# Turning q and k on VectorE in 32x32 blocks of bf16 pairs, and scores as four 32-row tiles of two half products

## Chip, cores and metric

The kernel runs on one core of one Trainium2 chip. The metric is device time in microseconds from start to end of one execution; lower is better. A core has five engines that run at the same time and wait for each other through semaphores: PE (TensorE, matrix products, with its weight loads shown apart as PEld), DVE (VectorE), ACT (ScalarE), POOL (GpSimd) and SP (SyncE, which here only issues DMAs).

## What is computed

Attention with a decay bias for 8 batches of 8 heads (576 positions, head width 64), then a token mixer and a channel mixer. `s` gives the decay. Cut to what matters:

```python
scores = scale * np.matmul(q, k.transpose(0, 1, 3, 2))        # q, k, v: (8, 8, 576, 64)
bias = -(cum[:, :, :, None] - cum[:, :, None, :])             # cum = cumsum(max(s, 0))
scores = np.where(causal, -1e9, scores + np.minimum(bias, 0.0))
attn = softmax(scores)
x = (attn @ v), heads side by side                            # (8, 576, 512)
h = np.maximum(x.T @ w_tok1, 0.0) @ w_tok2                    # 576 -> 256 -> 576
u = x + h.T
out = u + np.maximum(u @ w_ch1, 0.0) @ w_ch2                  # 512 -> 1536 -> 512
```

The kernel uses that the decay makes far keys negligible: each block of 128 queries meets only its own block of keys and the one before. Where a check at the end finds that the inputs do not allow this, a slower general path would run.

## The kernel before

**Units of work.** A batch has two *quads* of four heads. For each quad, k and q are loaded (L560), cast to bf16 (L573, on POOL in the steady part), turned so that the head width lies on partitions, and multiplied. A quad's four heads make two *pairs*. For each pair: two score blocks on PE (L650), an exponential on ACT for each block (L655, out of a PSUM tile of two banks, 128x1024 values), a causal mask on DVE (L660, L668), and two times nine small products with v (L685), a reciprocal (L692) and a scaling (L697) into `x`. When `x` of a batch is complete, the token mixer (L752, L773, with the addition L780) and the channel mixer (L826, the relu L833 or L835, L844, the addition L855) follow. From the third batch on, `u` is turned by a DMA transpose that SP issues (L789); for the first two batches PE turns it (L798).

**How q and k are turned.** PE does it: nine 128x128 transposes (L613) put k, then q, of a quad into a score tile of PSUM, and ACT (L623) or DVE (L625) copies each half out. Two heads of 64 rows then lie above each other in `kT` and `qT`, so a score block runs as two products of 64 rows at a time on the two halves of the array, each with the whole head width.

**What sets the order.** The kernel writes out its instructions through a planner of its own (class `Plan`, L47 to L202). Each operation is given a cost for each engine that may do it, a priority, the buffers it needs and what it waits for. The planner goes through time and picks for each engine the operation that can start first, by priority where several can. What it picks is the order of the instructions on that engine; on the chip each engine goes through its list in order. Buffers come from rings of few tiles: two PSUM tiles `psc` of two banks for scores, three `E` tiles, four `qkf` tiles for loads, two `qkn` tiles for casts. Loads are issued by SP in a fixed order among themselves (L419 to L421), between them the stores of the output (L860, L863) and the DMA transposes.

**Fills.** Where the planner leaves PE idle in its first 95 us, products with a zero tile are put in (L930), so that PE stays at work until the weights are there.

**Squares.** At the end a flag needs the sum of squares of q and k. For batches 2 to 7 it is taken from the cast tiles on ACT (L587), for batches 0 and 1 from a second load late in the run (L597).

Of the kernel before, what the change touches and what calls it, by code (L numbers as in the profile page):

```python
# [46 lines left out]
class Plan:  # L47
# [47 lines left out]
    def run(self, eps=0.03):  # L95
# [17 lines left out]
        def slot_time(o):  # L113
            t = 0.0
            want = {}
            for b in o.bufs:
                if b.slot is None:
                    r = b.ring
                    if b.ordered and r.queue[0] is not b:
                        return None  # L120
                    fr = [r.free[i] for i in range(len(r.tiles)) if not r.busy[i]]
                    if not fr:
                        return None
                    t = max(t, min(fr))
                    want[id(r)] = want.get(id(r), 0) + 1
            return t
# [207 lines left out]
def kernel(  # L334
# [12 lines left out]
    nc = tc.nc  # L347
# [13 lines left out]
    R = 9  # L361
    PR = S // R

# [29 lines left out]

    r_qf = ring("qkf", 4, [128, 2, R, D], FP32)
    r_qn = ring("qkn", 2, [128, 2, R, 2, D], BF16)
    r_qT = ring("qT", 2, [128, 2, S], BF16)
    r_kT = ring("kT", 2, [128, 2, 640], BF16)
# [21 lines left out]
    def load_op(fn, key, us):  # L419

        last[0] = P.op({"SP": (0.6, 0, fn)}, writes=key, prio=1, dma=us, after=last[0])  # L421
# [7 lines left out]
    def pads(eng, i):  # L429
        if i < 2:  # L430
            eng.memset(r_kT.tiles[i][:, :, S:640], 0.0)
        eng.memset(r_E.tiles[i][:, :, EW - 64 : EW], 1.0)
# [65 lines left out]
    NSQ = B * H // 2  # L498
    sq = sb("sq", [128, NSQ], FP32, fast)
    junk = sb("junk", [128, 2 * R * D], BF16, fast)  # L500
# [58 lines left out]
    def load_quad(f, src, b, qd):  # L559
        nc.sync.dma_start(out=f.t[:, :, :, :].rearrange("p a r d -> p a (r d)"),  # L560
                          in_=src[b, 4 * qd : 4 * qd + 4, :, :].rearrange("(a e) (p r) d -> (e p) a (r d)", a=2, r=R))

    def stage_qk(b, qd):
        n = Buf(r_qn)
        qkn[(b, qd)] = n
        for i, src in enumerate((k, q)):
            f = Buf(r_qf)
            load_op(lambda f=f, src=src: load_quad(f, src, b, qd), [(f, 0)], 256 * 0.113 / 16)

            def cast(e, i=i, f=f):  # L570
                o, a = n.t[:, i, :, :, :], f.t[:, :, :, :].rearrange("p a r d -> p r a d")
                if e == 0:
                    nc.gpsimd.tensor_copy(out=o, in_=a)  # L573
                elif e == 1:
                    nc.vector.tensor_copy(out=o, in_=a)
                else:
                    nc.scalar.copy(out=o, in_=a)  # L577
            alts = {"POOL": (*c_pool(1152, 0.0010), lambda cast=cast: cast(0))}
            if b == 0 and (qd, i) != (1, 0):
                alts["DVE"] = (0.82, 1.04, lambda cast=cast: cast(1))  # L580
                alts["ACT"] = (*c_act(1152), lambda cast=cast: cast(2))
            castop[(b, qd, i)] = P.op(alts, reads=[(f, 0)], writes=[(n, i)], prio=b * 10 + 4 * qd if b else 0)
        if b < 2:
            return
        for a in range(2):
            col = (b * 2 + qd) * 2 + a
            P.op({"ACT": (1.2, 1.6, lambda a=a, col=col: nc.scalar.activation(  # L587
                out=junk[:, :].rearrange("p (n d) -> p n d", d=D),
                in_=n.t[:, :, :, a, :].rearrange("p t r d -> p (t r) d"), func=AF.Square,
                accum_out=sq[:, col : col + 1]))}, reads=[(n, 0), (n, 1)], writes=[("sq", col)], prio=60)  # L590

    def stage_sq(b, qd):
        for i, src in enumerate((k, q)):
            f = Buf(r_qf)
            load_op(lambda f=f, src=src: load_quad(f, src, b, qd), [(f, 0)], 256 * 0.113 / 16)
            col = (b * 2 + qd) * 2 + i
            P.op({"ACT": (1.2, 1.6, lambda f=f, col=col: nc.scalar.activation(  # L597
                out=junk[:, :], in_=f.t[:, :, :, :].rearrange("p a r d -> p (a r d)"), func=AF.Square,
                accum_out=sq[:, col : col + 1]))}, reads=[(f, 0)], writes=[("sq", col)], prio=60)
# [3 lines left out]
    def quad(b, qd):  # L603
        nat = qkn[(b, qd)]
        pads = [("pad", 1)] if b == 0 and qd == 1 else []
        qT, kT = Buf(r_qT), Buf(r_kT)
        for ti, dst in ((0, kT), (1, qT)):
            pt = Buf(r_sc, False)

            def tr(ti=ti, pt=pt):  # L610
                o = pt.t[:, :, :].rearrange("p a n -> p (a n)").bitcast(BF16)
                for r in range(R):
                    nc.tensor.transpose(out=o[:, r * 128 : (r + 1) * 128],  # L613
                                        in_=nat.t[:, ti, r, :, :].rearrange("p a d -> p (a d)"), identity=ident[:, :])
            P.op({"PE": (R * 0.056, R * 0.056 + 0.3, tr)}, reads=[(nat, ti)] + pads, writes=[(pt, 0)], holds=[dst],
                 prio=(b * 4 + qd * 2, 2))
            for e in range(2):
                def ev(eng, e=e, pt=pt, dst=dst):
                    o = dst.t[:, e, 0:S].rearrange("d (p r) -> d p r", r=R)
                    i = pt.t[:, :, :].rearrange("p a n -> p (a n)").bitcast(BF16)[:, 0 : R * 128]  # L620
                    i = i.rearrange("d (r e p) -> d e p r", r=R, e=2)[:, e, :, :]
                    if eng == 0:
                        nc.scalar.copy(out=o, in_=i)  # L623
                    else:
                        nc.vector.tensor_copy(out=o, in_=i)  # L625
                P.op({"ACT": (*c_act(576), lambda ev=ev: ev(0)), "DVE": (*c_dve(576), lambda ev=ev: ev(1))},
                     reads=[(pt, 0)], writes=[(dst, e)], prio=1)
        for e in range(2):
            pair(b, qd, e, qT, kT)

    def pair(b, qd, e, qT, kT):
        np_ = b * 4 + qd * 2 + e
        E = Buf(r_E)
        odd = b % 2
        pads = [("pad", np_)] if 0 < np_ < 3 else []
        h = 4 * qd + e
        for gi, group in enumerate(([(0, 0, 256), (1, 128, 384)], [(2, 256, 512), (3, 384, 576), (4, 512, 576)])):
            ps = Buf(r_sc, False)
# [6 lines left out]
            def mm(ps=ps, cols=cols):  # L645
                for (jc, a, z, c0) in cols:
                    j0 = S - 128 if odd and jc == NJ - 1 else jc * 128
                    for hh in range(2):
                        p0 = hh * 64
                        nc.tensor.matmul(out=ps.t[:, hh, c0 : c0 + z - a], lhsT=kT.t[p0 : p0 + 64, e, j0 : j0 + 128],  # L650
                                         rhs=qT.t[p0 : p0 + 64, e, a:z], start=True, stop=True)
            P.op({"PE": (0.34, 0.64, mm)}, reads=[(kT, e), (qT, e)] + pads, writes=[(ps, 0)], holds=[E], prio=(np_, 1))

            def ex(ps=ps, gi=gi):
                nc.scalar.activation(out=E.t[:, :, gi * 512 : gi * 512 + 512], in_=ps.t[:, :, :], func=AF.Exp, scale=0.125)  # L655
            P.op(act(1024, ex), reads=[(ps, 0)], writes=[(E, jc) for (jc, a, z) in group], prio=0)

            def mk(gi=gi):
                o = E.t[:, :, gi * 512 : gi * 512 + 512].rearrange("p e (c n) -> p e c n", c=2)[:, :, :, 0:128]
                nc.vector.tensor_tensor(out=o, in0=o, in1=keep[:, :].unsqueeze(1).unsqueeze(1).to_broadcast([128, 2, 2, 128]),  # L660
                                        op=ALU.mult)
            keys = [(E, 2 * gi), (E, 2 * gi + 1)]
            P.op({"DVE": (0.45, 0.65, mk)}, reads=keys, writes=keys, prio=0)
            if gi == 1:
                def mk4():
                    k0 = 64 if odd else 0
                    o = E.t[:, :, EB[4] : EB[4] + 64]
                    nc.vector.tensor_tensor(out=o, in0=o, in1=keep[:, k0 : k0 + 64].unsqueeze(1).to_broadcast([128, 2, 64]),  # L668
                                            op=ALU.mult)
                P.op({"DVE": (0.22, 0.42, mk4)}, reads=[(E, 4)], writes=[(E, 4)], prio=0)  # L670
# [5 lines left out]
        for hh in range(2):  # L676
            pa, rc = Buf(r_mx if b == 0 and hh else r_av, False), Buf(r_rc, False)

            def av(pa=pa, hh=hh):
                o = pa.t[:, 0 : NJ * 66].rearrange("p (c n) -> p c n", n=66)  # L680
                for ic in range(NJ):
                    j_lo = max(ic - 1, 0)
                    for jc in range(j_lo, ic + 1):
                        d0 = ewin(jc, ic, odd)
                        nc.tensor.matmul(out=o[:, ic, 0 : D + 1], lhsT=E.t[:, hh, d0 : d0 + 128],  # L685
                                         rhs=vp.t[:, jc, h + 2 * hh, 0 : D + 1], start=(jc == j_lo), stop=(jc == ic))
# [8 lines left out]
            def nrm(pa=pa, rc=rc, hh=hh):  # L695
                o = pa.t[:, 0 : NJ * 66].rearrange("p (c n) -> p c n", n=66)
                nc.vector.tensor_tensor(  # L697
                    out=x.t[:, :, (h + 2 * hh) * D : (h + 2 * hh + 1) * D], in0=o[:, :, 0:D],
                    in1=rc.t[:, :].unsqueeze(2).to_broadcast([128, NJ, D]), op=ALU.mult)
            P.op(dve(330, nrm), reads=[(pa, 0), (rc, 0)], writes=[(x, h + 2 * hh)], prio=0)  # L700
# [33 lines left out]
    def tok(b):  # L734
# [31 lines left out]
        for c in range(NJ):  # L766
# [20 lines left out]
            if b >= 2:  # L787
                def trd(dst=dst, di=di, tc_=tc_):
                    nc.sync.dma_start_transpose(out=uT.t[:, :, tc_ * 128 : tc_ * 128 + 128], in_=dst.t[:, di, :])  # L789
                P.op({"SP": (0.6, 0, trd)}, reads=rk, writes=[(uT, c)],  # L790
# [21 lines left out]
    def chan(b, u, us, uT):  # L812
# [26 lines left out]
        for ci, c in enumerate((4, 0, 1, 2, 3) if odd else (0, 1, 2, 3)):  # L839
# [24 lines left out]
            P.op({"SP": (0.6 if c < NJ - 1 else 1.2, 0, st)}, reads=[(o, 0)], prio=0, dma=128 * 0.088 / 16)  # L864
# [79 lines left out]
    need = nc.values_load(flagi[0:1, 0:1], min_val=0, max_val=4096)  # L944
# [34 lines left out]
```

## Time and profile before

| what | value |
|---|---|
| median of 14 runs | 328.46 us (324.63 to 331.49) |
| the profiled execution's own time | 332.11 us |
| its span on the core | 330.3 us |
| PE busy | 306.1 us, 93% of the span |
| PEld (weight loads, beside PE) | 174.3 us, 53% |
| ACT busy | 186.2 us, 56% |
| DVE busy | 179.4 us, 54% |
| POOL busy | 84.8 us, 26% |
| DMA queue of SP | 68432 packets, 46.17 MB, 50.6% of 16 engines |
| TensorE clock granted over the span | 0.978 |

Busy shares are means over the span. A matmul is reported with its whole passage through the array, so consecutive matmuls overlap in the table: the time that one takes from the next is the distance between their starts, and it is read from the chain or the timeline, not from the mean duration. The page also gives the span in 40 slices with a digit for each engine, the chain of work that ended last, and the costliest groups of instructions by line. "Idle before, releaser" is time in which an engine stood still ahead of that line and what ended it.

### The profile page before, as it was taken

Reading aid. Unit: us, or ns where it says so; the run is one execution under the profiler, and the core shown is the slowest. Engines: PE = TensorE matmul, PEld = TensorE weight load, DVE = VectorE, ACT = ScalarE, POOL = GpSimd, SP = SyncE. Lnnn points to the kernel's source line nnn. Section 1 sums busy time; section 2 is a strip of 40 time slices with the busy share of each in tenths; the row PEclk is TensorE's granted clock in tenths of the full one; section 3 lists DMA queues with packets and bytes.
Section 4 is the critical chain, followed back from the end, with each engine's and each line's share of the span. In section 5 each row is a group of like instructions: output and inputs, shape, how many; then the busy total and the mean of one; then the engine's idle time right before and its main releaser. Section 6 shows DMA issues by size and latency. Waiting matters only on the chain.

```text
span 330.3 us, 6344 instructions
## 1 busy us (share of the span) xinstructions
PE 306.1 (93%) x2490; PEld 174.3 (53%) x2525; DVE 179.4 (54%) x406; ACT 186.2 (56%) x299; POOL 84.8 (26%) x110
## 2 busy tenths in 40 slices
PE   7895989998999999998999999998899999999991
PEld 3453566565675454544665454545574455447640
DVE  5857570779951656484735547574584645430020
ACT  3761475399884739552973748656884238207500
POOL 3194078319225200531145020802000000000000
PEclk9997899999999999999999999999799999999997
DMA  7999999899910597197502794478501410051031
GB/s 215 256 227 207 207 285 230 261 254 317 253 50 2 116 282 256 36 257 175 172 2 51 161 297 147 134 192 249 207 2 31 125 70 2 16 154 40 1 99 70
DMA packets 71880, 50.43 MB, mean 153 GB/s; under 512 B 53985, under 2 KB 56417, under 8 KB 71841
## 3 DMA queue, kind: packets, MB, share of 16 engines
q1 hardware_dynamic: 68432, 46.17, 50.6%
q0 software_dynamic: 3408, 3.77, 6.9%
q8 instruction: 22, 0.36, 0.5%
q14 instruction: 18, 0.14, 0.1%
HBM read 40.71 MB, written 9.44 MB: 152 GB/s over the span
## 4 chain that ended last, share of the span: by engine, by line
PE 72%; DVE 5%; DMA 4%; ACT 2%; issue 1%; ACTq 0%; SPq 0%
PE pmx L826 27%; PE pmx L844 26%; PE psc L650 4%; PE pav L685 4%; PE pmx L752 4%; PE pmx L773 4%; PE psc L613 3%; DMA qkf<-in_k_dram 3%; DVE ub L780 1%; DVE E L660 1%; DMA uTb<-us 1%; ACT junk L597 1%; DVE qT L625 1%; DVE E L668 1%; ACT E L655 1%
## 5 line engine op out<-in xcount | busy, mean ns | idle before, releaser
L826 PEld LDWEIGHTS <-wc 128*128 128x128 bf16 x624 | 58.5, 99 | 33.7 <-issue 3.0
L655 ACT ACTIVATE E<-psc 128x1024 bf16<-128x1024 f32 x64 | 63.0, 1024 | 22.9 <-PE psc L650 22.4
L826 PE MATMUL pmx<-uTb,wc 128*128 128x320 bf16 x384 | 58.0, 304 | 1.5 <-DMA uTb<-us 1.3
L844 PE MATMUL pmx<-wc,gb 128*128 128x512 bf16 x232 | 54.7, 379 | 0.5 <-issue 0.2
L573 POOL CAST qkn<-qkf 128x1152 bf16<-128x1152 f32 x29 | 33.2, 1163 | 70.7 <-PE psc L613 42.3
L544 POOL TENSOR_TENSOR vp<-vf,wT 128x512 bf16<-128x512 f32 (+1 forms) x35 | 36.4, 1060 | 56.7 <-PE pav L685 23.6
L826 PE MATMUL pmx<-uTa,wc 128*128 128x512 bf16 (+1 forms) x234 | 44.6, 336 | 1.6 <-DVE ga L835 1.1
L844 PE MATMUL pmx<-wc,ga 128*128 128x512 bf16 x182 | 44.5, 379 | 0.5
L833 ACT ACTIVATE gb<-pmx 128x320 bf16<-128x320 f32 x66 | 28.7, 437 | 25.1 <-PE pmx L826 17.8
L660 DVE TENSOR_TENSOR E<-E,keep 128x512 bf16<-128x512 bf16 x64 | 32.8, 516 | 9.0 <-ACT E L655 8.9
L833 ACT ACTIVATE ga<-pmx 128x512 bf16<-128x512 f32 (+1 forms) x45 | 22.8, 507 | 24.5 <-PE pmx L826 23.7
L844 PEld LDWEIGHTS <-gb 128*128 128x128 bf16 x240 | 22.3, 98 | 25.3 <-issue 0.4
L685 PEld LDWEIGHTS <-E 128*128 128x128 bf16 x576 | 25.6, 98 | 15.5 <-DVE E L660 3.4
L685 PE MATMUL pav<-vp,E 128*128 128x65 bf16 x540 | 27.1, 194 | 4.6 <-DVE E L660 3.0
L697 DVE TENSOR_TENSOR x<-pav,rc 128x320 bf16<-128x320 f32 x60 | 29.4, 490 | 1.9
L844 PEld LDWEIGHTS <-ga 128*128 128x128 bf16 x192 | 17.8, 98 | 19.7 <-issue 0.3
L587 ACT ACTIVATE junk<-qkn 128x1152 bf16<-128x1152 bf16 x24 | 28.0, 1165 | 0.1
L650 PE MATMUL psc<-qT,kT 64*128 64x256 bf16 (+2 forms) x320 | 24.0, 252 | 3.2 <-ACT qT L623 1.8
L855 DVE TENSOR_TENSOR of<-pmx,ua 128x512 f32<-128x512 f32 x16 | 11.1, 691 | 23.4 <-PE pmx L844 13.6
L613 PE MATMUL psc<-ident,qkn 128*128 128x128 bf16 x288 | 21.0, 219 | 2.1 <-ACT qkn L577 2.1
L650 PEld LDWEIGHTS <-kT 64*128 64x128 bf16 x320 | 11.8, 94 | 20.3 <-issue 16.6
L692 DVE RECIPROCAL rc<-pav 128x5 f32<-128x5 f32 x60 | 11.4, 190 | 19.0 <-PE pav L685 18.8
(86 smaller groups left out, 290.2 us busy)
## 6 DMA issues: line engine op xcount, KB each, us to landing
qkf<-in_k_dram SPq DMA_DIRECT2D x20, 576.0 KB, 5.4
qkf<-in_q_dram SPq DMA_DIRECT2D x20, 576.0 KB, 6.2
vf<-in_v_dram SPq DMA_DIRECT2D x32, 256.0 KB, 6.7
out_dram<-of SPq DMA_DIRECT2D x32, 256.0 KB, 3.0
wc<-in_moe_w_ch_dram POOLq DMA_DIRECT2D x8, 384.0 KB, 10.7
vf<-in_v_dram SPq DMA_DIRECT2D x8, 128.0 KB, 4.2
out_dram<-of SPq DMA_DIRECT2D x8, 128.0 KB, 2.4
w<-in_moe_w_tok_dram POOLq DMA_DIRECT2D x2, 256.0 KB, 4.9
```

The source lines that it names most:

```text
L544: eng.tensor_tensor(out=vp.t[p0 : p0 + n, c, :, 0:D], in0=vf.t[p0 : p0 + n, c, :, :], in1=wT[p0 : p0 + n, cw, b * H : b * H + H].unsqueeze ...
L573: nc.gpsimd.tensor_copy(out=o, in_=a)
L587: P.op({"ACT": (1.2, 1.6, lambda a=a, col=col: nc.scalar.activation(out=junk[:, :].rearrange("p (n d) -> p n d", d=D), in_=n.t[:, :, :, a, ...
L613: nc.tensor.transpose(out=o[:, r * 128 : (r + 1) * 128], in_=nat.t[:, ti, r, :, :].rearrange("p a d -> p (a d)"), identity=ident[:, :])
L650: nc.tensor.matmul(out=ps.t[:, hh, c0 : c0 + z - a], lhsT=kT.t[p0 : p0 + 64, e, j0 : j0 + 128], rhs=qT.t[p0 : p0 + 64, e, a:z], start=True ...
L655: nc.scalar.activation(out=E.t[:, :, gi * 512 : gi * 512 + 512], in_=ps.t[:, :, :], func=AF.Exp, scale=0.125)
L660: nc.vector.tensor_tensor(out=o, in0=o, in1=keep[:, :].unsqueeze(1).unsqueeze(1).to_broadcast([128, 2, 2, 128]), op=ALU.mult)
L685: nc.tensor.matmul(out=o[:, ic, 0 : D + 1], lhsT=E.t[:, hh, d0 : d0 + 128], rhs=vp.t[:, jc, h + 2 * hh, 0 : D + 1], start=(jc == j_lo), st ...
L697: nc.vector.tensor_tensor(out=x.t[:, :, (h + 2 * hh) * D : (h + 2 * hh + 1) * D], in0=o[:, :, 0:D], in1=rc.t[:, :].unsqueeze(2).to_broadca ...
L826: nc.tensor.matmul(out=pm.t[:, 0 : e - a], lhsT=wc1[:, m, cc * 128 : cc * 128 + 128], rhs=uT.t[:, m, a:e], start=(m == 0), stop=(m == NMC ...
L833: lambda cc=cc, pm=pm, a=a, e=e: nc.scalar.activation(out=g.t[:, cc, a:e], in_=pm.t[:, 0 : e - a], func=AF.Relu),
L844: nc.tensor.matmul(out=pm.t[:, :], lhsT=g.t[:, cc, c * 128 : c * 128 + 128], rhs=wc2[:, cc, :], start=(cc == 0), stop=(cc == NCC - 1))
```

## The change

It replaces the way in which q and k are turned, and what follows from the new layout.

- **Load.** Each quad of k or q comes with four DMAs instead of one, one for each head, into its own 32 partitions. A partition holds nine pieces of 512 bytes (two consecutive positions of 64 fp32 values) instead of pieces of 2304 bytes. The planner's cost of an SP issue is set from 0.6 to 0.42, of a DMA transpose from 0.6 to 1.25, of a store from 0.6 to 0.45.
- **Cast.** As before, but contiguous; k and q have separate tiles, four in the ring.
- **Turn.** One DVE transpose for k and one for q of a quad. It regards two bf16 values as one 32-bit word and turns each 32x32 block of words. Afterwards a head occupies 32 partitions; partition d holds the values 2d and 2d+1 of each position side by side. There is no PE transpose of q and k, no PSUM tile for it and no copy out of PSUM.
- **Scores.** Each head's product is two half products (even values, odd values) accumulated in PSUM, each over 32 rows, with operands that step over every other bf16 value. The four heads of a quad sit on four row groups. A block of a quad writes both `psc` tiles and takes two `E` tiles at once. In batch 0 a block is still made of two heads only.
- **Planner.** `slot_time` allows an operation to take two tiles of one ring.
- **Squares.** Taken of the contiguous cast tile or load; 32 of them as before.

The diff, cut to its core:

```diff
-                    if b.ordered and r.queue[0] is not b:
+                    n = want.get(id(r), 0)
+                    if b.ordered and (len(r.queue) <= n or r.queue[n] is not b):
                         return None
...
-    R = 9
-    PR = S // R
+    R = 2
...
-    r_qf = ring("qkf", 4, [128, 2, R, D], FP32)
-    r_qn = ring("qkn", 2, [128, 2, R, 2, D], BF16)
-    r_qT = ring("qT", 2, [128, 2, S], BF16)
-    r_kT = ring("kT", 2, [128, 2, 640], BF16)
+    r_qf = ring("qkf", 4, [128, S * 2], FP32)
+    r_qn = ring("qkn", 4, [128, S * 2], BF16)
+    r_qT = ring("qT", 2, [128, S, 2], BF16)
+    r_kT = ring("kT", 2, [128, 640, 2], BF16)
...
-        last[0] = P.op({"SP": (0.6, 0, fn)}, writes=key, prio=1, dma=us, after=last[0])
+        last[0] = P.op({"SP": (0.42, 0, fn)}, writes=key, prio=1, dma=us, after=last[0])
...
-    def load_quad(f, src, b, qd):
-        nc.sync.dma_start(out=f.t[:, :, :, :].rearrange("p a r d -> p a (r d)"),
-                          in_=src[b, 4 * qd : 4 * qd + 4, :, :].rearrange("(a e) (p r) d -> (e p) a (r d)", a=2, r=R))
+    def load_quad(src, b, qd):
+        f = Buf(r_qf)
+        for g in range(4):
+            load_op(lambda g=g: nc.sync.dma_start(
+                out=f.t[32 * g : 32 * g + 32, :].rearrange("p (k n) -> p k n", n=R * D),
+                in_=src[b, 4 * qd + g, :, :].rearrange("(k p r) d -> p k (r d)", p=32, r=R)),
+                [(f, g)], S / R * 0.027 / 16)
+        return f
...
     def quad(b, qd):
...
-                for r in range(R):
-                    nc.tensor.transpose(out=o[:, r * 128 : (r + 1) * 128],
-                                        in_=nat.t[:, ti, r, :, :].rearrange("p a d -> p (a d)"), identity=ident[:, :])
...
-                P.op({"ACT": (*c_act(576), lambda ev=ev: ev(0)), "DVE": (*c_dve(576), lambda ev=ev: ev(1))},
-                     reads=[(pt, 0)], writes=[(dst, e)], prio=1)
...
+        for i, dst in ((0, kT), (1, qT)):
+            n = qkn[(b, qd, i)]
+            P.op(dve(576, lambda n=n, dst=dst: nc.vector.transpose(
+                out=dst.t[:, 0:S, :].rearrange("d t e -> d (t e)").bitcast(FP32).rearrange(
+                    "d (k p r) -> d k r p", p=32, r=R),
+                in_=n.t[:, :].bitcast(FP32))), reads=[(n, 0)] + (pads if i == 0 else []), writes=[(dst, 0)], prio=1)
...
-            def mm(ps=ps, cols=cols):
+            def mm(heads, pss=pss, cols=cols):
                 for (jc, a, z, c0) in cols:
                     j0 = S - 128 if odd and jc == NJ - 1 else jc * 128
-                    for hh in range(2):
-                        p0 = hh * 64
-                        nc.tensor.matmul(out=ps.t[:, hh, c0 : c0 + z - a], lhsT=kT.t[p0 : p0 + 64, e, j0 : j0 + 128],
-                                         rhs=qT.t[p0 : p0 + 64, e, a:z], start=True, stop=True)
-            P.op({"PE": (0.34, 0.64, mm)}, reads=[(kT, e), (qT, e)] + pads, writes=[(ps, 0)], holds=[E], prio=(np_, 1))
+                    for e in range(2):
+                        for g in heads:
+                            rows = slice(32 * g, 32 * g + 32)
+                            nc.tensor.matmul(out=pss[g // 2].t[:, g % 2, c0 : c0 + z - a], lhsT=kT.t[rows, j0 : j0 + 128, e],
+                                             rhs=qT.t[rows, a:z, e], start=(e == 0), stop=(e == 1))
+            if b == 0:
+                for e in range(2):
+                    P.op({"PE": (0.5, 0.8, lambda e=e, mm=mm: mm((2 * e, 2 * e + 1)))},
...
+            else:
+                P.op({"PE": (0.65, 0.95, lambda mm=mm: mm((0, 1, 2, 3)))}, reads=[(kT, 0), (qT, 0)],
+                     writes=[(pss[0], 0), (pss[1], 0)], holds=Es, prio=(np_, 1))
...
-                P.op({"SP": (0.6, 0, trd)}, reads=rk, writes=[(uT, c)],
+                P.op({"SP": (1.25, 0, trd)}, reads=rk, writes=[(uT, c)],
```

## The prediction

> **What bounds the kernel now.** I read the page's slices first, then a table by stage, the chain that ended last, and last the timeline of PE around one score block.
>
> ```profile
> PE   7895989998999999998999999998899999999991
> DVE  5857570779951656484735547574584645430020
> ACT  3761475399884739552973748656884238207500
> ```
>
> PE stands at 9 in nearly every slice after the start, the others at 4 to 8. The table by stage (window in us, its length, then busy us and instruction counts of PE, PEld, DVE, ACT and POOL, then clock, DMA share and GB/s) says where that holds:
>
> ```profile
> 0.00:54.00 54.00, 44.11 (x389) 27.67 (x395) 32.77 (x74) 30.63 (x47) 25.99 (x48) 0.94 1.01 236
> 54.00:85.00 31.00, 28.91 (x304) 17.32 (x308) 22.72 (x49) 20.36 (x32) 18.90 (x19) 1.00 0.95 263
> 85.00:298.00 213.00, 207.52 (x1654) 114.50 (x1674) 120.13 (x280) 124.71 (x199) 39.90 (x44) 0.99 0.48 131
> 298.00:330.30 32.30, 25.51 (x152) 14.77 (x151) 3.81 (x6) 10.49 (x24) 0.00 (x0) 0.93 0.16 53
> ```
>
> To 54 us the DMA engines are full and 16.2 us of PE's time is fills; to 85 us there are still 2.7 us of fills. From 85 to 298 us PE is 97% busy with no fill, DMA at half: here PE time is run time. The last 32 us are mixer only. The groups that the change touches, by line (count, busy us, mean ns, then idle before and its releaser):
>
> ```profile
> L613 PE MATMUL psc<-ident,qkn 128*128 128x128 bf16 x288 | 21.0, 219 | 2.1 <-ACT qkn L577 2.1
> L650 PE MATMUL psc<-qT,kT 64*128 64x256 bf16 (+2 forms) x320 | 24.0, 252 | 3.2 <-ACT qT L623 1.8 <-DVE qT L625 1.2
> L625 DVE COPY kT<-psc 128x576 bf16<-128x576 bf16 x14 | 10.5, 754 | 6.4 <-ACT kT L623 6.3
> ```
>
> Of the 288 transposes, 171, that is 19 groups of nine, start between 85 and 298 us. In the chain in order of time a group takes 0.50 us of PE:
>
> ```profile
> 177.84 0.50 PE psc L613 x9
> 178.34 0.86 PE pmx L773 x4
> ```
>
> A score block costs more than it streams. Timeline of PE (start, length, line, tile, count):
>
> ```profile
> 185.73 0.59 PE L844 MATMUL pmx<-wc,gb 128*128 128x512 bf16 x2
> 186.26 0.39 PE L650 MATMUL psc<-qT,kT 64*128 64x256 bf16 x4
> 186.58 0.44 PE L685 MATMUL pav<-vp,E 128*128 128x65 bf16 x9
> 186.96 0.40 PE L650 MATMUL psc<-qT,kT 64*128 64x256 bf16 x6
> ```
>
> Two L844 at 0.215 us each (four of 512 columns take 0.86 us in the chain) end their turn at 186.16; the block starts at 186.26 and L685 only at 186.58. So a block takes 0.42 us, of which 512 columns at 0.42 ns stream for 0.21; about 0.1 goes ahead of it and 0.1 after. Two blocks in a row (ten matmuls) take 0.64.
>
> [...] The trace shows two of 64 rows together (their 1024 columns in 0.21 us), nothing of four. [...] The trace shows loads that keep up with nine L685 matmuls in 0.26 us, 29 ns each, all contiguous; a stepped load isn't in it. [...] No DVE transpose is in the trace; the nearest row is L625, 576 elements in 0.754 us.
>
> **The change, part by part**, against the profiled execution (span 330.3, own time 332.1 us). The median of the runs is 328.46, 3.65 below it; I take differences from the profile and subtract them from the median.
>
> *PE transposes removed.* In the full stretch 19 x 0.505 = 9.6 us of path. In 54 to 85 us another 7 groups, 3.5 us; but there the change's order of instructions has 32 fills where the old one has 9, so the plan found nothing to put there. I count 1 us of it (0 to 4). Before 54 us nothing: fills cover PE, and DMA sets the pace.
>
> *Score blocks.* In the full stretch lie 11 quads, 44 blocks: 8 doubles at 0.644 and 28 singles at 0.425 make 17.05 us. After, a quad has two blocks, 22 in all, each with one pair of gaps, 0.19. Streaming: each row group does 512 columns twice, 0.43 us, if four run at once. Issue: 16 and 24 pairs of load and matmul; at the 29 ns of L685 they need 0.46 and 0.70. Lower bound 22 x 0.62 = 13.7 (gain 3.3), upper 11 x (0.65 + 0.89) = 17.0 (gain 0). I take the middle, a gain of 1.7.
>
> *Evacuations gone, DVE transposes added.* ACT loses 38 copies, 23.8 us; DVE loses 26, 19.6 us, and gains 32 transposes. At 0.75 each that is 24 us; at double, 48. DVE at 54% of the span has room for either, so it costs nothing while q and k are turned before PE asks: the cover is the mixer matmuls, over ten us for each quad. If it is late, the price is one transpose pair, 1.5 us per quad. The turn is shorter as a chain (two transposes, 1.5 us, against 0.5 + 0.65 + 0.76 us twice, partly beside each other), which speaks against that.
>
> *A stall that goes.* Around 229 us PE waits for the qT copies, which stand on ACT behind a square that waits for its load:
>
> ```profile
> 228.95 1.25 PE L826 MATMUL pmx<-uTb,wc 128*128 128x320 bf16 x8 [0.28 <-ACT gb L833]
> 231.95 0.40 PE L650 MATMUL psc<-qT,kT 64*128 64x256 bf16 x4 [1.75 <-ACT qT L623]
> 232.74 0.40 PE L650 MATMUL psc<-qT,kT 64*128 64x256 bf16 x6 [0.40 <-DVE qT L625]
> ```
>
> 2.2 us for the copies. The turn leaves ACT, but relus and exponentials stay behind the same square, and would be late next. I count 1 us (0 to 2.2).
>
> *Loads.* 40 loads of 256 packets become 160 of 288. Packets in this trace take 18 ns at 256 bytes and 93 ns at 2304; on that line 512 bytes take 27, so a load costs 1152 x 27 / 16 = 1.94 us of all engines instead of 72.65 / 40 = 1.82. If a packet costs like two of 256 bytes, 36 ns, it is 2.6. Six such loads are issued ahead of the mixer weights while DMA is full: 0.7 us at 27 ns, 4.7 at 36. I take +1. SP issues 120 more DMAs at about 0.4 us, 48 us in all; behind them in its queue stand v loads, stores and the DMA transposes of `u` (1.22 us each, for which L826 waited 1.4 us at 154 us). SP has no other work, and its row of waits holds far more than that; the loads are issued many us ahead. Nothing is added for it in the full stretch.
>
> *A wait that is added.* A block of a quad needs both `psc` tiles and two `E`; before, one of each. The second block of a quad stands in PE's queue until two exponentials (2.05 us) have read both tiles, with all later mixer matmuls behind it; in the new order about 2.2 us of other matmuls stand between. A square (1.17 + 0.20 us) ahead of the exponentials makes PE wait 1.4 us. Bound: none of 22 blocks, or half of them for 0.7 on average, 7.7 us. I take 2. Relief below nothing I exclude: the old blocks waited for one tile, no less.
>
> Sum: -9.6 - 1.7 - 1 - 1 + 1 + 2 = -10.3 us. The profiled execution would take 321.8, the median 318.2; I say 318.
>
> **Rivals.**
> *The new waits eat it*: the last item at its upper bound, and the 54 to 85 us stretch and the stall give nothing: -11.3 + 1 + 7.7 = -2.6, 326 us. For: 28 squares lie in that stretch on ACT. Against: ACT is relieved of 13 us there, and its idle before L655 is 20 us already.
> *Stepped weight loads are slow (slower than before)*: one mechanism, in the score blocks. Before, a quad costs (9.6 + 17.05) / 11 = 2.42 us of PE; after, 0.39 + 40 loads. It decides at 51 ns a load. [...]at 60 ns +4 and 333. For: no stepped load is in the trace. Against: [...]64-row loads take 94 ns, like 128-row ones, 3 ns apart.
> *It doesn't do what it says*: four tiles run two by two. Then a block streams 0.86 us: 22 x 1.05 = 23.1 us against 17.05, and the sum is -9.6 + 6.1 - 1 - 1 + 1 + 2 = -2.5, 326; with the added waits at their bound it is +3.2, 332. Against: the banks and row groups of the four heads differ, as those of the two do now.
> *More than I count*: blocks at their lower bound, all of the stall, 3.5 us in 54 to 85, no new wait: -9.6 - 3.3 - 3.5 - 2.2 + 1 = -17.6, 311.
>
> **Chances.** My forecast (313 to 323) 50%; more gain (307 to 313) 10%; waits (323 to 331) 20%, of it 12 faster, 6 within, 2 slower; two by two 6%, of it 2 faster, 2 within, 2 slower; slow loads 14%, all slower. A run of this kernel can tell about 0.5%. So faster 74%, same 8%, slower 18%. The range 310 to 330 leaves out the slow loads and the lower half of the larger gain, some 20%.
>
> **What would show it.** Right: no L613 group; in the full stretch 22 score blocks of 0.62 to 0.9 us with gaps of 0.1 around each; DVE transposes near 0.75 us; PE still 97% busy, its stretch some 10 us shorter. Wrong: PE idle ahead of score blocks released by ACT; score matmuls more than 51 ns apart on average; the first L826 of batch 0 several us after 40.7 us; transposes above 1.5 us with PE waiting on qT or kT.

## The result, and the profile after

The kernel after takes 332.75 us (median of 10 runs, 330.43 to 334.25), the kernel before 328.42 us in the same comparison (47 runs): a ratio of 1.0197, with a 95% interval of 1.0167 to 1.0226. Ratios here leave out executions more than 1.5% above the fastest of the same kernel, so a ratio isn't the quotient of the two medians. It is slower by some 2%, where 318 us was forecast and 310 to 330 was the range. The profiled execution has a span of 332.0 us and a granted clock of 0.965 (before 330.3 and 0.978).

The slices of the page, PE as shown of before, then the granted clock and the share of the DMA engines:

```profile
PE   6798999979799991999899998979999999999992
...
PEclk9599999999799997699999999999999999999998
DMA  8999999999999999997697279874300530042031
```

PE now has a hole: a 1 in the sixteenth slice, 124 to 133 us, and a clock of 7 and 6 tenths in it and in the next. DMA is at 9 up to some 150 us; in the kernel before it was full to 85 us and half busy from there. The table by stage, of after and then, with the same columns, two rows of before, into which its row of 85 to 298 us splits:

```profile
0.00:54.00 54.00, 47.23 (x420) 29.19 (x427) 29.49 (x76) 26.81 (x40) 21.89 (x44) 0.94 1.16 199
54.00:85.00 31.00, 27.27 (x292) 14.57 (x296) 24.19 (x51) 14.14 (x19) 16.14 (x16) 1.00 1.12 222
85.00:150.00 65.00, 55.44 (x463) 31.25 (x468) 36.34 (x77) 39.64 (x65) 27.35 (x29) 0.89 1.11 208
150.00:298.00 148.00, 141.50 (x1226) 76.38 (x1242) 90.42 (x195) 77.46 (x122) 20.84 (x23) 1.00 0.51 115
298.00:332.00 34.00, 27.41 (x161) 15.60 (x161) 4.15 (x6) 10.49 (x24) 0.00 (x0) 0.96 0.20 64
```

```profile
85.00:150.00 65.00, 64.53 (x526) 35.72 (x529) 38.48 (x92) 41.54 (x67) 17.67 (x20) 1.00 0.57 152
150.00:298.00 148.00, 142.99 (x1130) 78.78 (x1145) 81.64 (x188) 83.17 (x132) 22.23 (x24) 0.99 0.45 121
```

In 85 to 150 us, where PE was to be 97% busy, it is busy for 55.4 of 65 us at a clock of 0.89, and the DMA share is 1.11 where it was 0.57. (At 1.11 of 16 engines' time, packets of one engine overlap, so a packet's time is the time that it is under way.) After 150 us PE is the bound again, busy for 141.5 of 148 us. So there are two stretches with different signs. The first weight load of the channel mixer (L826 before, L823 after) of each batch says how much each is worth, in us:

| batch | 0 | 1 | 2 | 3 | 4 | 5 | 6 | 7 |
|---|---|---|---|---|---|---|---|---|
| before | 40.7 | 85.3 | 121.7 | 153.4 | 192.8 | 225.6 | 267.9 | 297.2 |
| after | 38.6 | 89.3 | 132.6 | 164.7 | 201.1 | 235.2 | 271.0 | 299.0 |

Up to batch 2 the kernel after loses 10.9 us. From there to batch 7 it needs 166.4 us instead of 175.5 and wins 9.1 back.

The groups that replaced those shown of before (no L613 is left), and a score block in the timeline of PE:

```profile
L628 PE MATMUL psc<-qT,kT 32*128 32x256 bf16 (+2 forms) x640 | 23.8, 253 | 3.6 <-ACT E L647 3.0
...
L628 PEld LDWEIGHTS <-kT 32*128 32x128 bf16 x640 | 15.8, 93 | 15.5 <-issue 14.2
L607 DVE STREAM_TRANSPOSE kT<-qkn 128x576 f32<-128x576 f32 x16 | 12.4, 773 | 6.5 <-ACT qkn L585 3.6 <-PE psc L628 2.2 <-POOL qkn L581 0.7
...
L607 DVE STREAM_TRANSPOSE qT<-qkn 128x576 f32<-128x576 f32 x16 | 12.1, 756 | 2.3 <-POOL qkn L581 2.2
```

```profile
165.77 0.71 PE L823 MATMUL pmx<-uTb,wc 128*128 128x320 bf16 x4
166.41 0.64 PE L628 MATMUL psc<-qT,kT 32*128 32x256 bf16 x16
166.97 2.89 PE L823 MATMUL pmx<-uTb,wc 128*128 128x320 bf16 x20
```

Four L823 of 320 columns take their turn in 0.53 us, to 166.30; the block starts at 166.41 and the next matmul at 166.97. The whole block of four heads takes 0.67 us with its two gaps. Its 16 matmuls have 4096 columns, which at 0.42 ns each would take 1.7 us one after the other, and 0.86 two by two (my estimate). So four 32-row tiles do run together, and a stepped load of 32 rows lasts 93 ns, no longer than the others (98 to 99 ns for the 128-row loads of the mixers and of L682, 94 for the 64-row loads before).

Where the hole comes from is in SP's queue. First PE around it, then SP (start, length of the issue, lines, count):

```profile
123.16 2.76 PE L841 MATMUL pmx<-wc,gb 128*128 128x512 bf16 x12
132.67 1.44 PE L823 MATMUL pmx<-uTa,wc 128*128 128x512 bf16 x3 [6.75 <-DMA uTa<-ua]
```

```profile
106.63 2.35 SPq L562 DMA_DIRECT2D qkf<-in_k_dram  x4
109.36 2.31 SPq L562 DMA_DIRECT2D qkf<-in_q_dram  x4
111.97 7.56 SPq L535 DMA_DIRECT2D vf<-in_v_dram  x5
119.62 2.06 SPq L562 DMA_DIRECT2D qkf<-in_k_dram  x4
121.78 2.13 SPq L562 DMA_DIRECT2D qkf<-in_q_dram  x4
124.59 1.20 SPq L860 DMA_DIRECT2D out_dram<-of  x2
126.11 5.25 SPq L786 DMA_TRANSPOSE uTa<-ua  x4
```

PE waits 6.75 us for batch 2's `u`, turned by four DMA transposes. The sums that they read (L777) end near 115.7 us, but SP, which works in order, is by then at the `v` loads, 1.5 us each, then at eight narrow loads and two stores, and reaches the transposes only at 126.11. In the kernel before, the same four went out at 107.91, ahead of all five `v` loads:

```profile
107.91 5.26 SPq L789 DMA_TRANSPOSE uTa<-ua  x4
...
114.36 4.88 SPq L535 DMA_DIRECT2D vf<-in_v_dram  x3
...
120.33 2.27 SPq L535 DMA_DIRECT2D vf<-in_v_dram  x2
```

The five hold SP for 7.2 us there too, so their length is not what is new; that the transposes stand behind them is. The chain that ended last has the same story (start, length, what):

```profile
107.31 5.33 DMA qkf<-in_k_dram
...
114.04 3.66 SPq L535
...
121.23 5.38 DMA qkf<-in_k_dram
...
130.16 2.43 DMA uTa<-ua
132.58 0.09 issue
132.67 1.44 PE pmx L823 x3
```

And the wait is not the whole loss: the granted clock is at 0.50 from 128 to 138 us, and the three matmuls at 132.67 take 1.44 us where the same three take 0.81 at full clock (shown below, at 121.98 us of another kernel).

### The profile page after: what moved, and what is told of

It is laid out like the page before. It is cut to its first block, busy times and chain, and to the rows that moved or that the text cites. A ratio compares the mean times of both kernels' runs of the same rounds, so it can differ in the third digit from the quotient of the medians.

```text
span 332.0 us, 6640 instructions
## 1 busy us (share of the span) xinstructions
PE 298.9 (90%) x2557; PEld 167.0 (50%) x2593; DVE 184.6 (56%) x404; ACT 168.5 (51%) x269; POOL 86.2 (26%) x110
## 4 chain that ended last, share of the span: by engine, by line
PE 42%; DMA 27%; SPq 12%; DVE 9%; issue 4%; POOL 3%; ACT 1%; POOLq 0%; ACTq 0%; DVEq 0%
PE pmx L823 18%; PE pmx L841 14%; DMA qkf<-in_q_dram 10%; DMA qkf<-in_k_dram 6%; SPq L535 6%; SPq L562 5%; DMA wc<-in_moe_w_ch_dram 3%; DMA vf<-in_v_dram 3%; PE pmx L749 3%; PE pav L682 3%; DMA w<-in_moe_w_tok_dram 3%; DVE E L652 2%; PE psc L628 2%; POOL qkn L581 2%; PE pmx L770 2%
## 5 line engine op out<-in xcount | busy, mean ns | idle before, releaser
L823 PEld LDWEIGHTS <-wc 128*128 128x128 bf16 x624 | 59.1, 99 | 40.7 <-issue 11.7
L647 ACT ACTIVATE E<-psc 128x1024 bf16<-128x1024 f32 x64 | 62.1, 1020 | 29.9 <-PE psc L628 29.3
L823 PE MATMUL pmx<-uTb,wc 128*128 128x320 bf16 x384 | 56.7, 301 | 0.5 <-DMA uTb<-us 0.4
L823 PE MATMUL pmx<-uTa,wc 128*128 128x512 bf16 (+1 forms) x236 | 46.9, 347 | 7.2 <-DMA uTa<-ua 6.7
L830 ACT ACTIVATE gb<-pmx 128x320 bf16<-128x320 f32 x74 | 32.1, 439 | 34.0 <-PE pmx L823 29.4
L652 DVE TENSOR_TENSOR E<-E,keep 128x512 bf16<-128x512 bf16 x64 | 36.2, 572 | 14.1 <-ACT E L647 13.9
L682 PEld LDWEIGHTS <-E 128*128 128x128 bf16 x576 | 26.5, 99 | 15.8 <-issue 2.8
L830 ACT ACTIVATE ga<-pmx 128x512 bf16<-128x512 f32 (+1 forms) x43 | 22.0, 515 | 21.8 <-PE pmx L823 18.5
L682 PE MATMUL pav<-vp,E 128*128 128x65 bf16 x540 | 27.5, 195 | 3.2 <-DVE E L660 2.1
L927 PE MATMUL pmx<-zero 128*128 128x512 bf16 (+5 forms) x88 | 26.0, 426 | 2.7 <-DVE zero L424 1.2
L841 PEld LDWEIGHTS <-ga 128*128 128x128 bf16 x192 | 17.7, 98 | 21.3 <-issue 2.7
L628 PE MATMUL psc<-qT,kT 32*128 32x256 bf16 (+2 forms) x640 | 23.8, 253 | 3.6 <-ACT E L647 3.0
L628 PEld LDWEIGHTS <-kT 32*128 32x128 bf16 x640 | 15.8, 93 | 15.5 <-issue 14.2
```

The lines of the kernel that those rows point to most:

```text
L628: nc.tensor.matmul(out=pss[g // 2].t[:, g % 2, c0 : c0 + z - a], lhsT=kT.t[rows, j0 : j0 + 128, e], rhs=qT.t[rows, a:z, e], start=(e == 0) ...
L823: nc.tensor.matmul(out=pm.t[:, 0 : e - a], lhsT=wc1[:, m, cc * 128 : cc * 128 + 128], rhs=uT.t[:, m, a:e], start=(m == 0), stop=(m == NMC ...
L830: lambda cc=cc, pm=pm, a=a, e=e: nc.scalar.activation(out=g.t[:, cc, a:e], in_=pm.t[:, 0 : e - a], func=AF.Relu),
L841: nc.tensor.matmul(out=pm.t[:, :], lhsT=g.t[:, cc, c * 128 : c * 128 + 128], rhs=wc2[:, cc, :], start=(cc == 0), stop=(cc == NCC - 1))
L927: f.fn = lambda t=r.tiles[slots[0]], n=n: nc.tensor.matmul(out=t[:, 0:n], lhsT=zero[:, 0:128], rhs=zero[:, 0:n], start=True, stop=True)
```

## The experiments

My theory at this point: the loads are the cause. Per packet they cost more than I took, and they hold SP's queue and the DMA engines up to 150 us. Rivals: small pieces as such; narrow DMAs as such; the four issues on SP; VectorE's new work; the queue's order alone.

**Pieces of the old size, and larger.** The kernel after with nine or eighteen tokens in a piece, the order of instructions unchanged:

```diff
-    R = 2
+    R = 9        # e1; 18 in e2
-                [(f, g)], S / R * 0.027 / 16)
+                [(f, g)], 288 * 0.027 / 16)
```

> The changed kernel with R = 9: the same four DMAs of 32 partitions for each load, in pieces of 2304 bytes instead of 512, and the same order of instructions on every engine. Packet theory (a 512-byte packet takes 43 ns where 27 were assumed, so the loads cost 123 us of all 16 engines instead of 73, and PE starves while DMA is full): about 318 us, the SP queue's share back from 68% to about 51%, no 7 us wait of L823 at 125 us. Issue theory (four DMAs of 32 partitions instead of one of 128 are the cost, by SP's time or by how they spread): at least 330. Order theory (blocks of four heads wait for two tiles and two exponentials): 332, unchanged.

> The changed kernel with R = 18: pieces of 4608 bytes, 128 packets for each quad load, the same order of instructions. Packet theory: 315 to 319, like R = 9 or a little better. Issue theory: at least 330. Order theory: 332.

Measured: 331.82 us (323.96 to 334.38, 4 runs) and 331.27 (325.37 to 334.08, 4 runs), before 329.81: none of the eight executions reaches the 319 that the theory of packets allowed, and beyond that nothing can be told from so wide a spread. The traces tell something (that of e1 is of its slowest execution, 334.4 us). In e1 a packet has 2304 bytes as in the kernel before, and takes 148.5 ns on average instead of 112.8. So the size of the pieces is not all of the loads' price: all the queue's packets of q and k cost 95.6 us of 16 engines in e1, 94.2 in e2, 123.4 in the kernel after and 72.7 before. And batch 2's mixer starts at 135.5 and 129.8 us, 3 us to either side of the kernel after, with 28 us less of packets. Something else had become slower: the transposes on VectorE take 1.21 and 1.25 us instead of 0.76.

**The old kernel with the new loads.** e3 splits each load of the kernel before in four of 32 partitions, with packets unchanged; e4 uses pieces of 256 bytes instead and four DMAs of 64 partitions, and the copies out of PSUM follow the new order; e8 is e3 with the four issued in another order.

```diff
-        nc.sync.dma_start(out=o, in_=i)
+        for g in range(4):               # e8: (0, 2, 1, 3)
+            nc.sync.dma_start(out=o[32 * g : 32 * g + 32], in_=i[32 * g : 32 * g + 32])
```

> The kernel before with each load issued as four DMAs of 32 partitions, its packets of 2304 bytes unchanged. Packet theory: 328, no difference. Issue theory: slower, 334 or more. Order theory: 328.

> The kernel before with its loads of q and k in pieces of 256 bytes (2304 packets for a quad instead of 256), four DMAs of 64 partitions each; PE still turns q and k. At the 20 ns of the v packets the loads then cost 115 us of all engines instead of 73. Packet theory: slower by 6 to 15 us, 334 to 343, with PE waiting in the first 150 us. Issue theory: slower by as much as the split of the loads alone. Order theory: 328, unchanged.

> The kernel before with each q or k load as four DMAs of 32 partitions, as in e3_old_split4, but issued in the order 0, 2, 1, 3, so that DMAs that follow each other write different halves of the partitions. [...]packets of 2304 bytes come back from the 150 ns of e3 to 113 to 125 ns (112.8 in the kernel before), and the time to within 1% of the kernel before (325.5 to 331.5 us) where e3 was 335. If a narrow DMA is slow by itself, or four issues for one cost SP the time, packets stay at 145 to 150 ns and the time at 333 to 338.

Measured: e3 335.15 us, ratio 1.012 (1.0019 to 1.0222), packets of 2304 bytes at 150.4 ns. e4 347.18 us, ratio 1.0559 (1.0456 to 1.0663), 256-byte packets at 22.9 ns. So narrow loads (by 1 to 2%), and above all small pieces, slow the old kernel too, with none of the new PE or VectorE work in it; in e4 most of the loss is at the start, where batch 0's mixer comes at 51.5 us instead of 40.7, although VectorE's copies out of PSUM take 0.46 us there instead of 0.75. e8: 336.11 us, ratio 1.0237 (1.0172 to 1.0303), packets at 128.8 ns. The other order took away over half of what a packet had gained in price (from 150.4 down to 128.8, where the kernel before has 112.8), but not a microsecond of time: in the old kernel the mixers of batches 1 to 4 start no later than before in e3 (82.2, 119.3, 151.0, 192.8), and its loss lies after 193 us, around the stall at 229 us (PE waits 3.2 us for `qT` there instead of 1.8). There DMA time was not the bound, and the expectation that the time would come back with the packets failed.

**The order of the four loads in the kernel after.** Nothing else is changed, and every engine's order stays.

```diff
-        for g in range(4):
+        for g in (0, 2, 1, 3):
```

> The changed kernel with the four head loads issued in the order 0, 2, 1, 3 instead of 0, 1, 2, 3; pieces of 512 bytes, all else and the order of the plan the same. [...]the 512-byte packet falls from 43 ns towards 27 to 35 and the time by 3 to 8 us, to 325 to 330. If the narrow DMA is slow for another reason[...], nothing moves: 332.

Measured: 323.52 us (321.77 to 325.19, 4 runs), ratio to before 0.9877 (0.9803 to 0.995); 9 us off the kernel after, 10 by the ratios. Packets of 512 bytes take 37.6 ns instead of 42.8. SP and the stage of e5:

```profile
105.81 6.10 SPq L535 DMA_DIRECT2D vf<-in_v_dram  x5
112.01 3.06 SPq L562 DMA_DIRECT2D qkf<-in_k_dram  x4
115.17 1.89 SPq L562 DMA_DIRECT2D qkf<-in_q_dram  x4
117.24 1.20 SPq L860 DMA_DIRECT2D out_dram<-of  x2
118.55 5.26 SPq L786 DMA_TRANSPOSE uTa<-ua  x4
```

```profile
85.00:150.00 65.00, 61.58 (x507) 32.72 (x505) 42.21 (x82) 40.18 (x64) 26.11 (x27) 0.97 1.05 214
```

The same queue runs 7.6 us earlier, PE is busy 6 us more in the stage, and the mixers of batches 2 and 7 start at 125.1 and 286.8 us. The order sets a part of a packet's price (37.6 ns against 42.8 here, 128.8 against 150.4 in e8 and e3); why it does, no run shows. That the packets don't come down to 112.8 in e8 shows that the order is not all.

**One load for a quad.** e6 loads with one DMA over 128 partitions (pieces of 4608 bytes) and leaves the order of instructions as in the kernel after; e7 also gives the planner one issue, its DMA time and a longer transpose.

```diff
-    R = 2
+    R = 18
+        def whole():
+            nc.sync.dma_start(out=f.t[:, :], in_=src[b, 4 * qd : 4 * qd + 4, :, :].rearrange("g (p r) d -> (g p) (r d)", r=R))
```

> The changed kernel with R = 18, where the four heads of a quad lie evenly in memory, so that one DMA of 128 partitions with one contiguous piece of 4608 bytes each loads a quad; the order of instructions is that of the changed kernel (the three other issues are left empty). DMA theory (narrow DMAs and small pieces together put off the first three batches by 11 us, and the rest of the run is as much faster as forecast): SP queue's share 47 to 52%, the channel mixer of batch 2 starts at 120 to 124 us instead of 132.6, total 316 to 321. Rival (the new order of the first batches itself, with its waits on four heads, costs the 11 us): batch 2 still at 130 or later, total 327 to 332.

> As the kernel with one DMA for each load, but the planner knows it: one issue, 1.82 us of DMA for a load, 1.21 us for a DVE transpose, so it makes another order. DMA theory: within 3 us of the former, 314 to 321, and faster than the kernel before. Rival: 327 to 332.

Measured: 324.77 us, ratio 0.9889 (0.9854 to 0.9924), and 325.69 us, ratio 0.9918 (0.9896 to 0.9939). Packets cost 69.5 us of all engines in e6, less than in the kernel before, and yet batch 2's mixer starts at 129.4 (e7: 132.5), later than e5's 125.1 with 108.3 us of packets. DMA time alone therefore does not set it. In e6 PE waits on VectorE instead, whose transposes take 1.25 us as in e2: 4.2 us for `gb` (L831 there), 2.9 for `qT`, 4.2 for `E`.

**What stands in SP's queue.** e9 has batch 2's `u` turned by PE (16 matmuls, as batches 0 and 1 are) instead of by DMA; e11 is e9 with the loads' order of e5; e14 does it in the kernel before.

```diff
-            if b >= 2:
+            if b >= 3:
                 def trd(dst=dst, di=di, tc_=tc_):
```

> The kernel after with batch 2's u turned by TensorE instead of by DMA transposes, so that nothing that TensorE waits for stands behind loads in SP's queue at 112 to 126 us; TensorE gets 16 transposes more, about 2 us with their weight loads. If the 6.9 us wait at 126 us is a cost of the queue's order alone, the channel mixer of batch 2 starts at 125 to 128 us instead of 132.6, later batches keep the gain, and the time falls by 3 to 6 us, to 327 to 330. If the DMA engines are the bound in 85 to 150 us, the mixer of batch 2 starts earlier but TensorE waits for q, k or v of the next batches instead, batch 3 starts at 163 to 166 as in the kernel after (164.7), and the time is 332 to 334.

> e5_alternate (323.5 us) with batch 2's u turned by TensorE instead of by DMA transposes. In e5 the transposes were issued at 118.6 us with no long wait, so the queue's order should have nothing more to give: TensorE's 16 added transposes cost 1 to 2.5 us, 324 to 326. If the loads ahead of the transposes still held batch 2 back, its mixer starts before 124 us (125.1 in e5), and the time is 320 to 322.5.

> The kernel before with batch 2's u turned by TensorE instead of by DMA transposes, and nothing else. There the transposes of batch 2 wait for nothing on SP, so if e11's gain over e5 comes from loads that stand ahead of them, this gains nothing: TensorE's 16 added transposes cost 1 to 2.5 us, 328.5 to 331. If the edit gains by itself (128 fewer small packets, a freer SP), 324 to 326.5.

Measured: e9 330.08 us, ratio 1.0064 (1.0037 to 1.0091); the mixer of batch 2 still starts at 132.4, as after, because PE now waits 2.8 us at 116 to 120 us for exponentials that stand on ACT behind the square of a late load (in the chain, DMA for `k` to 115.2, then cast, square, exponential, score block at 119.78). But it has no wait of 6.75 us, its clock is at half for 3.4 us there instead of 10.2, and batch 3 starts 2.7 us earlier (162.0). e14 330.56 us, ratio 1.0108 (1.0068 to 1.0148): where nothing holds the transposes back, the edit costs 2 us by the medians and 3.5 by the ratio. So taking the 6.75 us wait away brings 2.7 us net by the medians (4.4 by the ratios), or some 5 to 8 before the edit's own cost. Late loads still hold batch 2 back. e11, on the same chip as e9, 320.06 us (318.08 to 320.36, 7 runs), ratio 0.9775 (0.9733 to 0.9818): 10 us from the order of the loads alone, and 3.5 less than e5. The numbers of its second reading came true, but not shown is its reason, that in e5 loads still held batch 2 back: PE never waits for `uTa` in e5. It waits 2.3 us for `gb` at 101.80, runs at half clock from 103.2 to 106.6 us (more on this under VectorE), and e11 has neither. It is the fastest version that the study settles. PE at batch 2 in e11:

```profile
112.05 10.09 PE L841 MATMUL pmx<-wc,gb 128*128 128x512 bf16 x46
121.98 0.81 PE L823 MATMUL pmx<-uTa,wc 128*128 128x512 bf16 x3
```

No wait is left there, and the mixer starts when it did in the kernel before (121.7).

The fairest pair of traces is e14 and e11. Both turn batch 2's `u` on PE, and the clock is full in both from 33 to 314 us, while the traced execution of the kernel before is at half clock for 6.8 us from 28.9 and for 3.4 us from 233.7. The mixers again, in us:

| batch | 0 | 1 | 2 | 3 | 4 | 5 | 6 | 7 |
|---|---|---|---|---|---|---|---|---|
| e14 | 38.3 | 81.5 | 119.4 | 151.2 | 189.2 | 222.0 | 262.4 | 291.8 |
| e11 | 37.3 | 82.7 | 121.8 | 151.3 | 187.7 | 220.1 | 255.4 | 283.3 |

With the loads' order mended the change loses 2.4 us up to batch 2 and wins 10.9 from there to batch 7. The medians, measured on two chips, differ by 10.5 us.

**VectorE.** e10 is e5 with six tokens in a piece (1536 bytes). e12 is e11 with each transpose issued twice, the second time with the same result. e13 is e11 with three tokens in a piece.

```diff
-            P.op(dve(576, lambda n=n, dst=dst: nc.vector.transpose(
+            P.op(dve(576, lambda n=n, dst=dst: [nc.vector.transpose(
...
+                in_=n.t[:, :].bitcast(FP32)) for _ in range(2)]), reads=...
```

> The kernel after with the four DMAs of a load in the order 0, 2, 1, 3 (as in e5_alternate, 323.5 us) and six tokens in a piece instead of two: 1536-byte packets, a third of the packets, and a write step of 24 bytes in VectorE's transposes. If DMA time still bounds 85 to 150 us in e5, the load's packets fall from 108 us of all 16 engines to about 75 to 80, batch 2's mixer starts at 121 to 123 us instead of 125.1, and the time is 319 to 322. If DMA no longer bounds it, the packets fall just the same, but the starts and the time stay, 323 to 325. VectorE's transposes lie between 0.76 us (8-byte step) and 1.21 us (36-byte step); if VectorE has no slack the time rises by up to 3 us, to 326.5.

> e11_alternate_batch2_on_pe (320.1 us) with each of VectorE's 32 transposes of q and k issued twice, the second writing the same values to the same place: 0.76 us more of VectorE each, 24.5 us in all, some 12 of them before batch 2's channel mixer; loads and all other orders unchanged. If VectorE's time is hidden, as the prediction took it, the mixer of batch 2 starts within 1 us of e11's 121.8 and the time is 319.5 to 321.5. If VectorE is next to bound up to batch 2, as e10 against e5 suggests (0.45 us more each cost about 6 us there), batch 2 starts at 126 to 132 and the time is 325 to 332.

> e11_alternate_batch2_on_pe with three tokens in a piece: packets of 768 bytes, two thirds as many, and a write step of 12 bytes in VectorE's transposes. By packets alone: 50 to 55 ns each, some 100 us of all engines instead of 110, batch 2 at 120 to 122, time 318 to 320.5. If the transposes already take 1.2 us at a 12-byte step and VectorE bounds, 325 to 330; at 0.76 us they cost nothing more.

Measured: e10 329.81 us, ratio 1.0046 (1.0003 to 1.009), 6 us more than e5 although its packets cost 84.9 us instead of 108.3. Its transposes take 1.2 us. e12 341.58 us (341.24 to 344.44, 6 runs), ratio 1.0466 (1.0402 to 1.053): 24.9 us more of VectorE cost 21.5 us of time, 17.7 of them before batch 2's mixer (139.5 against 121.8), where 20 of the 32 transposes lie. PE's two longest waits for VectorE in e12 (total, times, longest, us):

```profile
PE pmx L823 <- DVE gb L832: 6.4, 5, 4.0
PE psc L628 <- DVE qT L607: 4.9, 5, 1.7
```

So VectorE's time is not hidden in e12. In e11 it is busy for 58% of the span, and for 70% up to batch 2. But the 17.7 us are not all the copies' own time: in e10 and e12 POOL and VectorE meet in a way that they don't in e11. The timeline of e10:

```profile
100.64 5.22 POOL L544 TENSOR_TENSOR vp<-vf,wT 128x512 bf16<-128x512 f32 x5
...
101.84 6.48 DVE L652 TENSOR_TENSOR E<-E,keep 128x512 bf16<-128x512 bf16 x2
...
105.81 2.22 POOL L581 CAST qkn<-qkf 128x1152 bf16<-128x1152 f32 x2
...
108.77 1.22 PE L823 MATMUL pmx<-uTb,wc 128*128 128x320 bf16 x4 [3.98 <-DVE gb L832]
```

Two multiplications that take 0.42 us each elsewhere (the median of L652 in the kernel after) take 6.5 us here, 3.1 and 3.4, while POOL's instructions follow each other, and PE waits 4 us for what stands behind them. In e12 the same two take 6.48 us from 105.63, PE waits 4.0 us, and the clock is at half from 113.7 to 120.4 us; the wait and half of that time are some 7 of the 17.7 us (my estimate). The traces of e1, e2, e5 and e6 have the same meeting, each with a wait for `gb` of 2.3 to 4.0 us and a spell of half clock after it; the kernel after, e9, e11 and e13 have no such wait over 0.5 us. So where a slower transpose seemed to cost much (e1, e2, e6, e10, e12), a good part is this. What slows VectorE in the meeting is not shown; one multiplication lasts as long there as some three of POOL's instructions (five take 5.22 us). Such excess over 0.42 us on L652 and L660 (L660 and L668 before) adds up to 9 us in the kernel before, none of it after 85 us, and to 15 in the kernel after, over 10 of it after 88 us. A likely reason for the growth (my estimate) is that casts and `v` products that wait for late loads come to lie on the multiplications; no run isolates it, and e11, with earlier loads, still has 9 us after 88.

e13: 322.26 us (316.25 to 325.97, 6 runs), ratio 0.9864 (0.9782 to 0.9946), packets 47.4 ns, transposes 0.95 us. Its spread takes in that of e11; which of the two is faster can't be said. Its 20 transposes before batch 2 take 3.8 us more than e11's, and batch 2's mixer still starts at 120.3, with packets at 91.0 us of all engines instead of 109.9: without the meeting, a little more of VectorE did no harm.

## Why the prediction was wrong, step by step

- **The step that failed is the one on loads and on SP's queue**: "the loads are issued many us ahead. Nothing is added for it in the full stretch", and beside it the price of 27 ns a packet with 36 as its bound. Measured are 42.8 ns, 123.4 us of all engines instead of 72.7, and DMA stays full to 150 us instead of 85. I had put the whole cost at the start (+1, at most +4.7). There is none there: batch 0's mixer is 2.1 us earlier (and within 0.3 us of e14's). It comes in the stretch that I called full: 10.9 us up to batch 2. The line was drawn through 18 and 93 ns, the median packets of the trace, while the 72.65 us it was set against are made of means, 20.2 and 112.8 ns. A line through the means gives 32 ns (my estimate); 27 is what the fastest quarter of the new packets take. The rest is that both sizes came from loads over all partitions: loads of 32 partitions cost more (e3's 150.4 ns against 112.8), and more in the order 0, 1, 2, 3 than in 0, 2, 1, 3 at both sizes measured (150.4 against 128.8 ns in e3 and e8, 42.8 against 37.6 in the kernel after and e5). And SP's time was counted as its own 0.4 us an issue, not as what comes to stand ahead of the transposes: 7.6 us of `v` loads and 4.2 of narrow ones. e5 shows the loads' part by order alone, 9 us, and e9 the queue's, 2.7 net.
- **"DVE at 54% of the span has room for either, so it costs nothing"** is the second step, and it holds only in part. The duration was right (0.76 us against 0.75), with some luck: it was read from a copy that takes 0.46 us with another access pattern (e4), and the transposes themselves take 0.95 to 1.25 with larger output steps. But up to batch 2 the kernel before has 9 copies there, 6.8 us, and the kernel after 20 transposes, 15.3 us; e12 puts a price of some 1.1 us on each further us there (17.7 for 20 transposes), or 0.7 without the meeting with POOL; in e13, with fewer packets, 3.8 us more cost nothing. How the 10.9 us divide between these 8.5 us and the loads stays open: with the same transposes e5 reaches batch 2 7.5 us earlier and e11 10.8, so most of it can be had back without touching them; but the transposes removed from PE should have brought that stretch below the kernel before, and it is only level.
- **PE transposes removed, score blocks**: right. The groups are gone, and a block of four heads takes 0.67 us, within 0.62 to 0.9; 22 of them make 14.6 us instead of 17.05, a gain of 2.4 (forecast 1.7, up to 3.3). From batch 2 to 7 the kernel after wins 9.1 us and e5, whose clock is full there, 13.8 (161.7 us). Against e14, whose clock is full too, e5 wins 10.7, and that is the fairer number.
- **The stall at 229 us**: too small. From batch 5 to batch 6 the kernel before takes 42.3 us, the one after 35.8. Transposes and blocks of two quads account for some 2.2 of the 6.5; of the rest, 4.3 by this estimate, 1.9 is the half clock after the stall in the traced execution (0.91 in 222 to 240 us), for e14 has the same waits of 2.2 us with a full clock and takes 40.4. So the stall itself gave some 2.4 instead of 1: the whole of its 2.2.
- **54 to 85 us**: forecast -1; instead batch 1's mixer is 4.0 us later, with DMA full.
- **The added wait**: right, 3.0 us in four waits (forecast 2).
- **Rivals**: slow stepped loads and tiles two by two did not happen; the slower outcome came by a mechanism that none of them named. Its place and price could have been read: the text itself lists the DMA transposes behind the loads in SP's queue, and drops them.

With the loads' order mended the forecast's mechanism shows: 323.5 and, with batch 2's `u` off the queue, 320.1 us, 10.5 below e14, where the sum was -10.3. That the two agree so well is luck: the stall gave over 1 us more than its term and the stretch up to batch 2 took 2.4 back.

## What to carry to other kernels

A change that relieves the engine at the bound must be priced at its transfers as closely as there: the size of a packet, how many partitions a DMA covers, in what order narrow ones are issued, and what stands behind it in the same queue. A busy share over the span says nothing of slack in a stretch: doubling the operation in question, with the same result, prices it, once what the doubling brings about besides (here a meeting of two engines) is taken off. Where four narrow DMAs must be issued, try issuing them in the order 0, 2, 1, 3: it brought 9 to 10 us here, where late loads were the bound, and nothing in the old kernel (e8 against e3).

## What the runs showed of the hardware

- The same 576-word 32x32 transpose on VectorE takes 0.76 us when its output words lie 8 bytes apart, 0.95 at 12, 1.2 at 24 and 36, and 1.25 at 72 bytes (after, e13, e10, e1, e2).
- A load packet of 2304 bytes takes 112.8 ns in DMAs over all partitions, 150 in four of 32 issued in the order 0, 1, 2, 3, and 129 in the order 0, 2, 1, 3 (before, e3, e8); 512 bytes take 42.8 and 37.6 in the last two ways (after, e5).
- A VectorE multiplication of 0.42 us took over 3 us while POOL's instructions followed each other without a break (e10).
- Four score tiles of 32 rows run together, a block of four heads in 0.67 us with its gaps, and a weight load of 32 rows with a step takes 93 ns, no more than the 98 to 99 of 128 rows (after).
